# Which projection chains run beside the probability-times-V products, and when the first normalisation of a batch is put on VectorE

## The chip, the cores and the metric

The kernel runs on one core of one Trainium2 chip. The metric is device time in microseconds; the time before is the median of nine runs. One further run was recorded by the hardware profiler, and every view below comes from that run. The core has five engines with a queue of instructions each: TensorE (PE, with its weight loads shown apart as PEld), VectorE (DVE), ScalarE (ACT), GpSimd (POOL) and SyncE (SP, which here issues DMAs).

## The reference

Two independent problems, A and B, of the same shape, S = 2048 rows and D = 1024, 32 heads of 32, and a sliding window of 256 keys:

```python
qkv = (x @ wqkv).reshape(B, S, 3, H, Dh).transpose(2, 0, 3, 1, 4)
q, k, v = qkv[0], qkv[1], qkv[2]
scores = jnp.einsum("bhqd,bhkd->bhqk", q, k) * (Dh ** -0.5)
mask = (idx[:, None] - idx[None, :] >= 0) & (idx[:, None] - idx[None, :] < W)
p = softmax(jnp.where(mask, scores, -1e9))
o = jnp.einsum("bhqk,bhkd->bhqd", p, v)
return o.transpose(0, 2, 1, 3).reshape(B, S, D) @ wo
```

The two results are joined along the last axis. All inputs are bf16.

## The kernel before

**Work.** A group `g` is four heads (128 columns of Q or K), so there are 16 groups over both problems. Scores are made in units of 64 keys by 64 queries for the four heads at once, eight units to a *session*, which makes 152 sessions. A session (`session`) is a burst of score matmuls into one PSUM tile `st` of four banks (in array tiles of 32x64), then two exponentials on ScalarE, each over half of the banks (`exp(0)` and `exp(2)`, called "first half" and "second half" here), then masks on POOL (`diag`, and the far edge in place). There is one `st`, so the scores of the next session wait for both halves of this one.

Every second session (`PV_EVERY = 2`, the even ones from 4 on) is followed on TensorE by the products of probabilities with V for one to three blocks of 256 queries (`pv`), in array tiles of 128x32. A `pv` also multiplies by ones to get the row sums, and it reads a tile `both` that `edge` makes on VectorE by adding two masked pieces. The result sits in one of two PSUM buffers `acc` until it is normalised.

**A norm** is two pieces in a list `side`: a reciprocal of the sums (`rinv`), and then two shuffles, a multiplication into `oT` and for every second norm an OR into a running check word (`top`). `run_side` issues one piece. `finish_norm(keep)` issues pieces until no more than `keep` norms are open. It is called with 1 ahead of each `pv`, and with 0 in the session ahead of a session that has `pv` work. Otherwise `emit` issues a piece when its own rough clock of VectorE (`clock.dve`) is not ahead of TensorE's.

**Chains.** All dense products are *chains* that fill TensorE between sessions: `qk_steps` makes 512 columns of Q or K of a group (8 steps of N = 512), `v_steps` two blocks of V for two groups (16 steps of N = 256), `out_steps` a 128x512 piece of the output (8 steps of N = 512). A chain accumulates in one of two PSUM buffers `pp`, and its last step is followed by a copy out of PSUM on ScalarE or VectorE, whichever the rough clock has free first (`evacuate`). A chain has a first session in which it may start (`early`) and a session ahead of which it must be done (`late`); the list is sorted by `late`, `start_chain` takes the first that may start, `forced` finishes what is due, and `level` works out how much chain work each session gets so that the rest is spread evenly.

**Two forms of a step.** `by_columns` issues a step as one 128x128 matmul when `whole[0]` is true ("whole"), and otherwise as four matmuls of 32 columns each ("column-tiled"). `whole[0]` is false exactly in sessions with `pv` work, so that TensorE stays in the 128x32 tiling from `pv` through the chain work; it is true in the others. Line 197 is the whole form, line 201 the column-tiled one, line 511 the scores, 521 the exponentials, 559 the `edge` addition, 592 `pv`, 605 to 615 the norm, 220 and 222 the copies out of PSUM on ScalarE and VectorE.

**Order.** The order of instructions on each engine is that in which this program issues them; nothing reorders them afterwards.

Of the kernel before, what the change touches and what calls it, by code (L numbers as in the profile page):

```python
# [29 lines left out]
DG_BUFS = 5  # L30
X_AHEAD = 1
PV_EVERY = 2
VG = 2
NS_MM = 216.0
NS_ROW = 450.0
# [9 lines left out]
class _Cfg:  # L45
    def __init__(self, S, D):
        assert D % 512 == 0 and S % 512 == 0, (S, D)
        self.S, self.D = S, D
        self.CT = D // P
        self.T = D // P  # L50
        self.NB = S // P
        self.SC = S // 512
        self.NCH = D // 512
        self.NW = 512
        self.scale = float(DH) ** -0.5


class _Chain:
    def __init__(self, early, late, steps):
        self.early, self.late, self.steps = early, late, steps  # L60
        self.size = sum(ns for ns, _ in steps)


# [19 lines left out]
def _fast_path(ctx, tc, cfg, problems, outs, consts, certify):  # L83
# [5 lines left out]
    NP = NB // 2  # L89
    NM = NPROB * T // VG  # L90
    ones = consts["ones"]
# [81 lines left out]
    def new_wv(m):  # L173
        wv[m] = wvp.tile([P, CT, VG * P], BF16, name="wv")

    def load_wv(m, lo, hi, queue):
        pi, mm = divmod(m, T // VG)
        w_ = VG * P
        queue.dma_start(out=wv[m][:, lo:hi, :],
# [25 lines left out]
    whole = [True]  # L205
# [39 lines left out]
    def v_steps(m, b):  # L245
        pi = m // (T // VG)
        k, a = divmod(b, QB)
        st_ = {}
        steps = []
        w_ = VG * P  # L250
        for h in range(512 // w_):
            for ct in range(CT):
                def f(ct=ct, h=h):
                    if "pp" not in st_:
                        st_["pp"] = new_pp()
                        if (m, k) not in vts:
                            vts[(m, k)] = vp.tile([P, QB, w_], BF16, name="vt")
                    by_columns(st_["pp"], h * w_, (h + 1) * w_,
                               xT[(pi, k)][:, ct, (a + h) * P:(a + h + 1) * P],
                               wv[m][:, ct, :], ct == 0, ct == CT - 1)  # L260
                    clock.pe += NS_MM * w_ / 512.0
                    if ct == CT - 1 and h == 512 // w_ - 1:
                        evacuate(vts[(m, k)][:, a:a + h + 1, :],
                                 st_["pp"][:].rearrange("p (h w) -> p h w", w=w_))
                steps.append((NS_MM * w_ / 512.0, f))
        return steps
# [43 lines left out]
    def pv_time(g, p):  # L310
        return -(-(edge_time(g, p) + 1) // PV_EVERY) * PV_EVERY

# [83 lines left out]
    chains = []  # L396
    for g in range(G):
        for k in range(NQ):
            for which in (0, 1):
                if g == 0 and k == 0:  # L400
                    continue
                late = first_use(g, k, 1 - which) - (1 if g else 0)
                early = max(-(-(g - 1) * NE // SLOTS), landed("x", g // T, k), landed("wqk", g))
                chains.append(_Chain(early, late, qk_steps(g, which, k)))
    for m in range(NM):
        for b in range(0, NB, 512 // (VG * P)):
            k = b // QB
            early = max(0, landed("x", m * VG // T, k), landed("wv", m))
            if m > 1:
                early = max(early, pv_time(VG * (m - 1) - 1, min(2 * k + 2, NP - 1)) + 1)  # L410
            late = pv_time(VG * m, b // 2) if m or k else 1
            chains.append(_Chain(early, late, v_steps(m, b)))
    for pi in range(NPROB):
        final = pi == NPROB - 1
        for b in range(NB):
            k = b // QB
            for ch in range(cfg.NCH):
                early = max(pv_time(pi * T + T - 1, 2 * k + 1) + 1, landed("wo", pi, ch))
                late = FREE if final else wo_time[(pi + 1, ch)] - 1
                if not final and k < NPROB * NQ - (2 * NQ - 1):  # L420
                    late = pv_time((pi + 1) * T, 2 * (2 * NQ - 1 - NQ + k)) - 1
                steps = last_steps if (pi, b, ch) == (NPROB - 1, NB - 1, cfg.NCH - 1) else out_steps
# [10 lines left out]

    current = []

    def start_chain(now):
        for n, c in enumerate(chains):
            if c.early <= now:
                current.extend(chains.pop(n).steps)
                return True  # L440
        return False

    def run_side():
        cost, f, last = side.pop(0)
# [5 lines left out]
    def emit(now, budget):  # L450
        done = 0.0
        while (current or chains) and done < budget - 0.5 * (current[0][0] if current else NS_MM):
            if not current and not start_chain(now):
                break
            ns, f = current.pop(0)
            f()
            done += ns
            second_half(clock.pe > clock.act)
            if side and (clock.dve < clock.pe + 100.0 or len(side) > 8):
                run_side()  # L460
# [103 lines left out]
    def pv(g, p):  # L564
        pi, t = divmod(g, T)
        m, u = divmod(g, VG)
        k, h = divmod(p, QB // 2)
        dg = diags.pop((g, p))

        def old(us):  # L570
            return [(n * HALF, w_ * HALF, pts[s_][:, :, a * HALF:(a + w_) * HALF])
                    for s_, a, w_, n in runs(g, us)]

        mids = [old(parts(q - 1, q)) if q else [] for q in (2 * p, 2 * p + 1)]
        moves = []
        if p:
            moves += [(None, 2 * p - 2) + x for x in old(parts(2 * p - 2, 2 * p))]
            moves += [(None, 2 * p - 1) + x
                      for x in old(parts(2 * p - 1, 2 * p) + parts(2 * p - 1, 2 * p + 1))]
        moves += [(None, 2 * p, P + o, w_, src) for o, w_, src in mids[1]]  # L580
        moves += [(None, 2 * p + i, i * P, P, dg[:, :, i, :]) for i in range(2)]
        for i in range(2):
            moves += [(i, 0, 2 * P + o, w_, src) for o, w_, src in mids[i]]
        acc = ps_acc.tile([P, 512], F32, name="acc")
        clock.pe = max(clock.pe, clock.norms.pop(0))
        sums = edges.pop((g, p)) if p else dg
        moves += [(i, 0, 2 * P, P, sums[:, :, i, :]) for i in range(2)]
        for x, (h, j, o, w_, src) in enumerate(moves):
            for r in range(4):
                c = u * P + 32 * r  # L590
                lhsT = vts[(m, j // QB)][:, j % QB, c:c + 32] if h is None else ones[:, h, :]
                nc.tensor.matmul(acc[32 * r:32 * r + 32, o:o + w_], lhsT=lhsT,  # L592
                                 rhs=src[:, r, :], start=(x == 0), stop=(x == len(moves) - 1),
                                 tile_position=(0, 32 * r), skip_group_check=True)
            clock.pe += NS_PV * w_ / P
        if (pi, k) not in oTs:
            oTs[(pi, k)] = opool.tile([P, T, 512], BF16, name="oT")
        turn = g * NP + p
        wide = normp.tile([P, 256], F32, name="wide")
        pieces = []  # L600

        def f():
            if turn % 2 == 0:
                inverses[0] = normp.tile([P, 2, P], F32, name="rinv")
            nc.vector.reciprocal(out=inverses[0][:, turn % 2, :], in_=acc[:, 2 * P:3 * P])  # L605
        pieces.append((COST["rinv"], f, False))

        def f():
            for h in range(2):
                nc.vector.stream_shuffle(out=wide[:, h * P:(h + 1) * P], in_=inverses[0][:, turn % 2, :],  # L610
                                         mask=[16 * h] * 32)
            nc.vector.tensor_tensor(out=oTs[(pi, k)][:, t, (p % 2) * 256:(p % 2 + 1) * 256],  # L612
                                    in0=acc[:, 0:256], in1=wide[:], op=ALU.mult)
            if turn % 2:
                nc.vector.scalar_tensor_tensor(
                    out=top[:], in0=inverses[0][:].rearrange("p h q -> p (h q)").bitcast(I32),
                    scalar=IN_RANGE, in1=top[:], op0=ALU.bitwise_xor, op1=ALU.bitwise_or)
        pieces.append((COST["mult"] + (COST["or"] if turn % 2 else 0.0), f, True))
        n = max([i + 1 for i, x in enumerate(side) if x[2]], default=0)
        side[n:n] = pieces  # L620

    def finish_norm(keep=0):
        while sum(x[2] for x in side) > keep:
            run_side()
# [66 lines left out]
    for now in range(END):  # L691
        forced(now)
        whole[0] = not (due and due[0][0] <= now)
        session(now)
        while due and due[0][0] <= now:
            _, pg, pk = due.pop(0)
            finish_norm(1)
            pv(pg, pk)
        if due and due[0][0] == now + 1:
            finish_norm()  # L700
        while edges_due and edges_due[0][0] <= now:
            edge(*edges_due.pop(0)[1:])
        emit_all(now, level(now) - fixed[now])
# [230 lines left out]
```

## Time and profile before

| | |
|---|---|
| median of nine runs | 609.66 us (608.88 to 611.62) |
| the profiled execution, its own time | 610.67 us |
| its span in the profile | 608.9 us |
| TensorE matmul busy | 587.7 us, 97% |
| TensorE weight loads busy | 364.3 us, 60% |
| VectorE busy | 409.8 us, 67% |
| ScalarE busy | 412.1 us, 68% |
| GpSimd busy | 360.2 us, 59% |
| instruction fetches (queue q8) | 115 packets, 1.88 MB |

The profiled execution's time is 1.8 us above its span, which is what lies around the span. A matmul's duration in the profile is modelled and overlaps its neighbours, so a busy share of 97% does not mean that the array works at its peak for 97% of the time: the distance between the starts of two matmuls says what a step takes. Some matmul records are missing from the trace: 75 of the whole steps of N = 512 are in the program and not in the records, most of them the first one after a burst of scores.

### The profile page before, as it was taken

How to read it: one execution, taken by the hardware profiler on the slowest of the kernel's cores; microseconds unless marked ns; L12 is line 12 of the kernel's file. 1: busy time of each engine (PE TensorE's matmuls, PEld its weight loads, DVE VectorE, ACT ScalarE, POOL GpSimd, SP SyncE). 2: the span in 40 equal slices, each digit the busy share in tenths (PEclk: the TensorE clock that was granted, in tenths of full speed). 3: DMA queues.
4: the chain of work that ended last, by engine and by line, in shares of the span. 5: the costliest groups of instructions: out<-in, count | busy, mean ns of one | idle time of the engine just before them, and what ended most of it. 6: DMA issues, size and time to landing. Idle time of an engine off the chain costs nothing.

```text
span 608.9 us, 32535 instructions
## 1 busy us (share of the span) xinstructions
PE 587.7 (97%) x14364; PEld 364.3 (60%) x14439; DVE 409.8 (67%) x1144; ACT 412.1 (68%) x523; POOL 360.2 (59%) x918
## 2 busy tenths in 40 slices
PE   9999999999999999999999999999999999999996
PEld 6566566657655666665665766665555765555443
DVE  1288786887887867866577766766868776767200
ACT  3577867787778777786567766777767777765332
POOL 0477666766777676766466666665666666664000
PEclk9999999999999999999999999999999999999999
DMA  9915110111034102544211100112020030114222
GB/s 241 174 48 133 38 38 4 39 37 39 4 56 89 40 3 46 102 89 107 55 38 37 38 4 4 39 37 73 3 81 29 12 100 11 56 55 132 71 78 65
DMA packets 86820, 35.73 MB, mean 59 GB/s; under 512 B 65552, under 2 KB 86160, under 8 KB 86672
## 3 DMA queue, kind: packets, MB, share of 16 engines
q1 hardware_dynamic: 85632, 33.31, 22.4%
q8 instruction: 115, 1.88, 1.3%
q10 hardware_dynamic: 1040, 0.26, 0.2%
q14 instruction: 33, 0.27, 0.2%
HBM read 17.83 MB, written 8.39 MB: 43 GB/s over the span
## 4 chain that ended last, share of the span: by engine, by line
PE 65%; issue 1%; ACT 0%; DVE 0%; ACTq 0%
PE pp L197 31%; PE pp L201 19%; PE acc L592 8%; PE st L511 6%; ACT pt L521 0%; ACT osb L220 0%; DVE unsafe_i L888 0%; PE pp L887 0%; ACTq L220 0%; ACT kT L220 0%
## 5 line engine op out<-in xcount | busy, mean ns | idle before, releaser
L521 ACT ACTIVATE pt<-st 128x1024 bf16<-128x1024 f32 x304 | 302.2, 1026 | 107.0 <-PE st L511 56.4
L532 POOL TENSOR_SCALAR_AFFINE_SELECT diag<-pt 128x256 bf16<-128x256 bf16 x512 | 210.9, 436 | 196.4 <-ACT pt L521 179.9
L559 DVE TENSOR_TENSOR both<-diag,pt 128x512 bf16<-128x512 bf16 (+1 forms) x256 | 123.6, 525 | 55.1 <-PE acc L592 29.0
L545 POOL TENSOR_SCALAR_AFFINE_SELECT pt<-pt 128x512 bf16<-128x512 bf16 (+1 forms) x256 | 154.8, 623 | 0.0
L197 PE MATMUL pp<-xT,wqk 128*128 128x512 bf16 (+1 forms) x581 | 135.8, 373 | 6.5 <-issue 5.2
L605 DVE RECIPROCAL rinv<-acc 128x128 f32<-128x128 f32 x128 | 121.7, 951 | 26.8 <-PE acc L592 25.2
L201 PE MATMUL pp<-xT,wqk 128*32 128x512 bf16 x1608 | 97.1, 379 | 0.0
L197 PEld LDWEIGHTS <-wqk 128*128 128x128 bf16 x638 | 59.1, 98 | 62.3 <-issue 0.3
L197 PE MATMUL pp<-wo_sb,oT 128*128 128x512 bf16 (+1 forms) x349 | 77.7, 374 | 2.2 <-issue 1.6
L511 PEld LDWEIGHTS <-kT 32*64 32x64 bf16 x3904 | 41.8, 103 | 57.4 <-issue 55.8
L197 PE MATMUL pp<-wv,xT 128*128 128x256 bf16 x587 | 71.0, 273 | 0.4 <-issue 0.4
L511 PE MATMUL st<-qT,kT 32*64 32x64 bf16 (+4 forms) x3904 | 66.9, 236 | 1.6 <-issue 0.6
L610 DVE STREAM_SHUFFLE wide<-rinv 128x128 f32<-128x128 f32 x256 | 64.3, 296 | 0.0
L220 ACT CAST osb<-pp 128x512 bf16<-128x512 f32 (+1 forms) x61 | 35.4, 580 | 42.0 <-PE pp L197 28.7
L197 PEld LDWEIGHTS <-xT 128*128 128x128 bf16 x587 | 55.5, 98 | 11.9 <-issue 0.4
L201 PEld LDWEIGHTS <-wqk 128*32 128x32 bf16 x1608 | 42.0, 97 | 31.7 <-issue 0.4
L197 PEld LDWEIGHTS <-oT 128*128 128x128 bf16 x367 | 34.7, 98 | 39.6 <-issue 0.4
L201 PE MATMUL pp<-wv,xT 128*32 128x256 bf16 x1748 | 55.2, 273 | 2.3 <-issue 2.3
L612 DVE TENSOR_TENSOR oT<-acc,wide 128x256 bf16<-128x256 f32 x128 | 54.4, 425 | 4.4
L201 PEld LDWEIGHTS <-xT 128*32 128x32 bf16 x1748 | 46.2, 97 | 7.2 <-issue 3.3
L592 PE MATMUL acc<-pt,vt 128*32 128x128 bf16 (+2 forms) x1792 | 48.8, 223 | 0.0
L592 PEld LDWEIGHTS <-vt 128*32 128x32 bf16 x2816 | 43.5, 97 | 7.7 <-issue 0.4
(47 smaller groups left out, 387.4 us busy)
## 6 DMA issues: line engine op xcount, KB each, us to landing
out_dram<-osb SPq DMA_DIRECT2D x63, 128.0 KB, 1.9
wqk<-in_B_wqkv_dram SPq DMA_DIRECT2D x32, 128.0 KB, 3.3
wqk<-in_A_wqkv_dram SPq DMA_DIRECT2D x24, 128.0 KB, 3.0
wo_sb<-in_A_wo_dram SPq DMA_DIRECT2D x16, 128.0 KB, 2.8
wv<-in_B_wqkv_dram SPq DMA_DIRECT2D x16, 128.0 KB, 3.3
wo_sb<-in_B_wo_dram SPq DMA_DIRECT2D x16, 128.0 KB, 2.2
oT<-in_A_x_dram SPq DMA_DIRECT2D x4, 256.0 KB, 4.8
wv<-in_A_wqkv_dram SPq DMA_DIRECT2D x2, 512.0 KB, 5.6
```

Of the source, the lines that this page charges most:

```text
L197: nc.tensor.matmul(out[:, lo:hi], lhsT=lhsT, rhs=rhs, start=start, stop=stop, skip_group_check=True)
L201: nc.tensor.matmul(out[c:c + 32, lo:hi], lhsT=lhsT[:, c:c + 32], rhs=rhs, start=start, stop=stop, tile_position=(0, c), skip_group_check=True)
L220: nc.scalar.copy(out=out, in_=in_)
L511: nc.tensor.matmul(scores[c * HALF:(c + 1) * HALF, r, a * HALF:(a + w_) * HALF], lhsT=kT[rows, keys], rhs=qT[rows, q:q + w_ * HALF], start ...
L521: nc.scalar.activation(out=pt[:, lo:lo + 2, :n * HALF], in_=scores[:, lo:lo + 2, :n * HALF], func=ACT.Exp, bias=-SHIFT, scale=cfg.scale)
L532: nc.gpsimd.affine_select(out=diags[(g, p)][:, :, h, lo:lo + HALF], in_=pt[:, :, a * HALF:(a + 1) * HALF], pattern=[[0, 4], [1, HALF]], co ...
L545: nc.gpsimd.affine_select(out=blk, in_=blk, pattern=[[0, 4], [-1, w_ * HALF]], compare_op=ALU.is_gt, fill=0.0, base=-HALF * (us[a][2] - 3) ...
L559: nc.vector.tensor_tensor(out=both[:, :, h, o:o + w_], in0=dg[:, :, h, o:o + w_], in1=pts[t][:, :, a:a + w_], op=ALU.add)
L592: nc.tensor.matmul(acc[32 * r:32 * r + 32, o:o + w_], lhsT=lhsT, rhs=src[:, r, :], start=(x == 0), stop=(x == len(moves) - 1), tile_positi ...
L605: nc.vector.reciprocal(out=inverses[0][:, turn % 2, :], in_=acc[:, 2 * P:3 * P])
L610: nc.vector.stream_shuffle(out=wide[:, h * P:(h + 1) * P], in_=inverses[0][:, turn % 2, :], mask=[16 * h] * 32)
L612: nc.vector.tensor_tensor(out=oTs[(pi, k)][:, t, (p % 2) * 256:(p % 2 + 1) * 256], in0=acc[:, 0:256], in1=wide[:], op=ALU.mult)
```

## The change

A chain gets a mark, `dense`, which is set for V chains alone. When a chain is about to start, `start_chain` now looks at the session's form and at what is left of its budget. In a session with whole-array steps it wants a V chain as long as more than 900 ns of the budget are left, and otherwise one of the others; in a column-tiled session it is the other way round. If the first chain that may start is not of the wanted kind and is not due by the next session, the first one of the wanted kind that may start and is due within 14 sessions (`REACH`) is taken in its place. Apart from that, one call `finish_norm(1)` is put behind the `pv` batch of a session.

```diff
+REACH = 14
...
 class _Chain:
-    def __init__(self, early, late, steps):
-        self.early, self.late, self.steps = early, late, steps
+    def __init__(self, early, late, steps, dense=False):
+        self.early, self.late, self.steps, self.dense = early, late, steps, dense
...
-            chains.append(_Chain(early, late, v_steps(m, b)))
+            chains.append(_Chain(early, late, v_steps(m, b), dense=True))
...
-    def start_chain(now):
-        for n, c in enumerate(chains):
-            if c.early <= now:
-                current.extend(chains.pop(n).steps)
-                return True
-        return False
+    def start_chain(now, left):
+        able = [n for n, c in enumerate(chains) if c.early <= now]
+        if not able:
+            return False
+        pick = able[0]
+        want = whole[0] == (left > 900.0)
+        if chains[pick].late > now + 1 and chains[pick].dense != want:
+            pick = next((n for n in able if chains[n].dense == want
+                         and chains[n].late <= now + REACH), pick)
+        current.extend(chains.pop(pick).steps)
+        return True
...
-            if not current and not start_chain(now):
+            if not current and not start_chain(now, budget - done):
...
             _, pg, pk = due.pop(0)
             finish_norm(1)
             pv(pg, pk)
+        if not whole[0]:
+            finish_norm(1)
         if due and due[0][0] == now + 1:
             finish_norm()
```

## The prediction

> **What bounds the kernel now.** I read the chain of waits on the page first, then TensorE's groups by shape, then TensorE's timeline for the distance between starts, then the waits of the weight loads, and last VectorE's timeline wherever TensorE stood still.
>
> ```profile
> PE 65%; issue 1%; ACT 0%; DVE 0%; ACTq 0%
> ```
>
> The chain that ended last is TensorE's own work; no other engine holds 1% of it. So only two things count: what a TensorE step costs, and the places where TensorE stands still.
>
> The steps, in the order whole Q/K, whole V, column-tiled V, column-tiled Q/K:
>
> ```profile
> 200.64 1.89 PE L197 MATMUL pp<-xT,wqk 128*128 128x512 bf16 x8 [0.16 <-PE st L511]
> 202.37 0.93 PE L197 MATMUL pp<-wv,xT 128*128 128x256 bf16 x7
> ...
> 165.44 1.69 PE L201 MATMUL pp<-wv,xT 128*32 128x256 bf16 x53
> ...
> 293.69 2.00 PE L201 MATMUL pp<-xT,wqk 128*32 128x512 bf16 x32
> ```
>
> Columns: start, extent, what, how many. One V matmul lasts 273 ns in the profile, one of N = 512 379. Whole V: (930 - 273) / 6 = 109 ns a step. Column-tiled V: (1690 - 273) / 52 x 4 = 109 ns. Whole Q/K: (1890 - 379) / 7 = 216 ns. Column-tiled Q/K: (2000 - 379) / 31 x 4 = 209 ns (216 from start to start over all runs of such steps). The two forms cost the same. A change between score tiles and either form costs 92 to 94 ns, from starts, whatever chain follows.
>
> Now the places where TensorE stands still:
>
> ```profile
> PEld L201 <- issue: 4.1, 6, 1.3
> ...
> 204.76 0.93 PE L201 MATMUL pp<-wv,xT 128*32 128x256 bf16 x25
> 206.69 0.29 PE L201 MATMUL pp<-wv,xT 128*32 128x256 bf16 x3 [1.01 <-issue]
> ...
> 292.91 1.05 PE L201 MATMUL pp<-wv,xT 128*32 128x256 bf16 x31 [1.04 <-issue]
> ```
>
> "Issue" means that no semaphore held it. In TensorE's instruction order, the stop at 206.69 is 194 instructions past a multiple of 256. I measured the starts of all matmuls against the program's order: thirteen stops (101.8, 141.1, 154.4, 167.4, 206.7, 215.0, 234.6, 292.9, 303.1, 339.4, 405.9, 441.5, 522.8 us) lie at 194 or 195 past a multiple of 256, in V, scores and Q/K alike, and only the first has a semaphore too. Together they are 5.0 us. The DMA view between 203.32 and 206.69 us shows one packet on the instruction queue; all 115 packets are 16 KB or 256 instructions of 64 bytes. TensorE outran its instruction fetch.
>
> The other kind of stop is inside `pv`, eleven of them, together 2.8 us:
>
> ```profile
> 84.33 0.24 PE L592 MATMUL acc<-both,ones 128*32 128x128 bf16 x4 [0.18 <-DVE both L559]
> 84.87 0.24 PE L592 MATMUL acc<-both,ones 128*32 128x128 bf16 x4 [0.30 <-DVE both L559]
> ...
> 78.83 0.69 DVE L222 CAST vt<-pp 128x512 bf16<-128x512 f32 x1 [0.67 <-PE pp L201]
> 79.43 0.95 DVE L605 RECIPROCAL rinv<-acc 128x128 f32<-128x128 f32 x1
> ...
> 83.66 2.27 DVE L559 TENSOR_TENSOR both<-diag,pt 128x512 bf16<-128x512 bf16 x4
> ```
>
> `pv` waits for `both`, which VectorE makes late. One batch earlier VectorE sat 0.67 us on a copy whose chain was not done, with the first norm behind it; both norms then ran in the odd session ahead of the additions.
>
> **What the Trainium skill says.** "Runtime: NRT & Kernel Launch", section Instruction fetch mechanics: instructions stream in 16 KiB blocks of 256, the next fetched while the current one runs, the crossing "mostly hidden". The trace agrees on the block, but the crossing is not hidden where 256 instructions run in under about 3 us. "TensorE: Matmul & The Clock Gate", section Back-to-back issue gap: N / 2.4 + 2.5 ns, so 109 and 216; the trace agrees, in both forms. "TensorEngine Tiling (Array Packing)", Key Properties: a change of tiling drains the array (here 92 to 94 ns); its Restrictions: column tiling disables fast weight load. No rate here shows the latter, as the loads are hidden.
>
> **Part 1, the choice of chain.** The instruction orders of both kernels give the moves. V steps in whole form go from 587 to 772 of 1024, column-tiled from 437 to 252: 185 leave. Q/K column-tiled go from 402 to 500, output from 153 to 159: 104 enter. In plain step time this is worth nothing: 185 x (109 - 109) + 104 x (216 - 216). The changes of tiling stay as many.
>
> What it moves is instruction density. A column-tiled V step is 8 instructions in 109 ns, or 73 per us, a column-tiled Q/K step 37, a whole V step 18; `pv` is 146. TensorE loses 486 instructions. I added the durations of each block of 256 from boundary to boundary (109 and 216 per step, N / 2.4 + 2.5 by the number of tiles for scores and `pv`, 92 per change). Before, 16 blocks take under 3.0 us, and what all blocks lack of 3.25 us sums to 10.7 us; 5.0 us of that was really lost, since some fetches start early. After, 10 blocks are under 3.0, and the lack is 7.2. At the same share the loss is 7.2 x 5.0 / 10.7 = 3.4 us: **-1.7 us**. Bounds: -4 (the share falls, as fetches lie better) and +1.5 (as now at 292.9, where a block of 3.05 us lost 1.2 because its fetch began late).
>
> The choice also moves work in time. V chains come early, the sum of steps is up to 5.5 us ahead by session 20, and sessions 20 to 70 get less, about 0.11 us each and 0.22 from 57 to 69. The total is the same at session 70 and the order hardly differs from 140 on. A shorter session leaves ScalarE less room. Where a copy lies between the two halves, it needs 0.39 to the first half, 0.92 + 0.47 to the second, 1.03 for that and 0.05 back: 2.86 us, and more if the copy waits for its chain:
>
> ```profile
> 197.24 1.02 ACT L521 ACTIVATE pt<-st 128x1024 bf16<-128x1024 f32 x1 [0.61 <-ACT pt L521]
> 198.50 0.59 ACT L220 CAST vt<-pp 128x512 bf16<-128x512 f32 x1 [0.23 <-PE pp L201]
> 198.98 1.03 ACT L521 ACTIVATE pt<-st 128x1024 bf16<-128x1024 f32 x1
> ```
>
> Session 54 above is already bound: the next scores start at 200.06, 50 ns after the second half. Going through the sessions with these durations I get 0.47 us of such waits before (the trace has 0.45) and 0.85 after, in sessions 21, 23, 53, 54, 59, 63 and 69: **+0.4 us**, bounds 0.1 and 5.
>
> Third, chains other than V run closer to their use. Only one gets too close: K of group 0, block 3, is finished at the end of session 6 and read in the middle of the scores of session 7, 0.2 us after its last matmul. The like case today (Q block 1, session 1, 0.18 us) stops the scores for 0.65 us, so **+0.5 us**, bounds 0 and 0.8. All others keep 1.2 us or more. V of group pairs 2 to 4 starts 3 to 6 sessions sooner, in sessions 29, 47 and 66; the loads were issued at 63.7, 124 and 191 us, tens of us ahead, so SP's and POOL's queues hold nothing up.
>
> **Part 2, the norm behind the batch.** No work is added; the first of two norms moves ahead of the even session's addition and copies. It waits for the first `acc`, which is done half a batch (about 0.5 us) before; behind it wait an addition that is needed two sessions later, and copies, which go to ScalarE where the rough clock has VectorE behind. A norm is 1.86 us, 2.20 with its OR (200.82 to 203.02 in VectorE's timeline), an addition about 1.15. Between two batches VectorE then has 1.86 + 2.20 + 2 x 1.15 = 6.4 us against about 6.3 from the first `acc` to the use of `both`, with no copy to idle on. At each of the stops where two norms were open, the odd session's addition now has one norm in front instead of one and a half or two. I take 0.6 us of waits in place of 2.8: **-2.2 us**. Bounds: -2.8, and +1 if a late copy on VectorE keeps a `pp` buffer.
>
> **Sum.** -1.7 + 0.4 + 0.5 - 2.2 = -3.0. The profiled span goes from 608.9 to 605.9 and its own time from 610.67 to 607.7; the median shown is 1.0 below that run, so 606.7.
>
> **Rivals.** *ScalarE becomes the bound in sessions 20 to 70 (slower).* The shorter sessions fall under the chain first half, copy, second half. For it: today the margin there is often 50 to 300 ns and sessions lose 110 to 220. Against: only 20 sessions in the new order have a copy between the halves and are under 3.13 us. If all of them wait as copies do in session 54 (0.25 each), this costs 5.0 in place of 0.4, and the kernel ends 1.6 us slower, at 611.3. It decides from 3.4 us of such waits on, where the gain is gone.
>
> *Stops only change places (no change).* Which block is short depends on where boundaries fall, and a removed wait on `both` makes its block shorter: the blocks at 37, 75, 84 and 438 us were covered by such waits. Then fetch loses 5 again and some of the 2.2 comes back as fetch: 609.7. For it: the fetch at 292.9 was late for reasons outside TensorE. Against: the counted lack already has these blocks uncovered.
>
> *Nearly all stops go (much faster).* Fetch and `both` together are 7.8 us; with 7.0 of them gone and 0.9 paid, 603.6. Against: one block of 2.0 us remains in the new order.
>
> **Numbers.** My sum 0.52 (own range 604.5 to 608.4), much faster 0.12, no change 0.17, slower 0.19. About 0.2% (1.2 us) is what a measurement of this kernel can tell from no change. Faster takes 0.49 of the first and the 0.12: 0.61; same 0.03 + 0.14 = 0.17; slower 0.22, with the rest of the third. Range: 603.2, which takes in most of the much faster case, to 611.0, which leaves out the slower case's upper half.
>
> **What would show it.** Thirteen fetch stops fall to seven to ten, with 3 to 4 us; no stop of over 1 us in column-tiled V. Waits on `both` are under 1 us. VectorE's reciprocal follows `pv` with no copy ahead. A stop of about 0.5 us inside the scores near 44 us. Step distances stay at 109 and 216. I am wrong if whole V steps come out over 109 ns, if scores wait for ScalarE for over 2 us, or if the stops at block boundaries keep their 5 us.

## The result and the profile after

The changed kernel takes 607.31 us (median of ten runs, 606.39 to 608.15) against 610.31 us of the kernel before in the runs beside it: a ratio of 0.9951, 95% interval 0.9939 to 0.9964. The forecast was 3.0 us less, and 3.0 us less came. The profiled execution took 608.26 us with a span of 606.5 us. The same total hides a different split from the one forecast, so the match is in part luck (see below).

The page after, the chain that ended last and three groups (line numbers have moved by 1 to 8; columns as on the page before):

```profile
PE 58%; issue 2%; POOL 1%; DVE 1%; ACT 1%; ACTq 0%; POOLq 0%
...
L611 DVE RECIPROCAL rinv<-acc 128x128 f32<-128x128 f32 x128 | 121.8, 952 | 89.3 <-PE acc L598 89.3
...
L202 PE MATMUL pp<-xT,wqk 128*32 128x512 bf16 x2000 | 119.8, 379 | 0.1
L198 PE MATMUL pp<-wv,xT 128*128 128x256 bf16 x772 | 91.9, 273 | 1.4 <-issue 1.2
```

The chain that ended last is still TensorE's own work. The counts show that the change does what it says: 2000 column-tiled Q/K matmuls (500 steps) and 772 whole V steps. The reciprocal's line shows part 2. VectorE now sits in front of the reciprocal, waiting for the `acc` it reads, for 89.3 us in all (before: 25.2 of the 26.8 us that it idled there); the waiting that used to lie in front of the `both` additions (55.1 us, now 11.3) and of the copies (57.8, now 45.2) now lies in front of the norms. VectorE's timeline around a batch (start, duration, what, and in brackets the idle time before):

```profile
82.43 0.96 DVE L611 RECIPROCAL rinv<-acc 128x128 f32<-128x128 f32 x1 [1.76 <-PE acc L598]
...
84.31 0.95 DVE L611 RECIPROCAL rinv<-acc 128x128 f32<-128x128 f32 x1
...
86.62 1.42 DVE L565 TENSOR_TENSOR both<-diag,pt 128x512 bf16<-128x512 bf16 x4
```

Both norms start as soon as the first `acc` is there, with no copy ahead, and the additions follow. Inside `pv` only two waits on `both` are left, 0.49 us together, where there were eleven with 2.8.

The waits of the weight loads, though, show that one kind of stop has stayed:

```profile
PEld L202 <- issue: 5.2, 6, 1.8
PEld L198 <- issue: 1.5, 4, 0.6
```

TensorE's timeline holds the longest:

```profile
379.82 0.93 PE L202 MATMUL pp<-wv,xT 128*32 128x256 bf16 x27
382.23 0.61 PE L202 MATMUL pp<-wv,xT 128*32 128x256 bf16 x13 [1.48 <-issue]
```

No semaphore, column-tiled V, and 195 instructions past a multiple of 256. There are nine such stops in this execution with 4.9 us, where the forecast said 3.4. Two of them, here and at 291.13 us, are over 1 us and in column-tiled V, where the forecast had none.

The stop that was forecast for session 7 is there. All engines between 42.2 and 43.0 us:

```profile
42.20 0.32 PE L517 MATMUL st<-qT,kT 32*64 32x192 bf16 x12
...
42.32 0.58 ACT L221 CAST kT<-pp 128x512 bf16<-128x512 f32 x1 [0.90 <-PE pp L202]
...
42.96 0.32 PE L517 MATMUL st<-qT,kT 32*64 32x256 bf16 x8 [0.44 <-ACT kT L221]
```

The scores begin, meet a block of K whose copy has only just started, and lose 0.61 us, measured between the starts of matmuls.

All runs side by side. "Own time" is that of the profiled execution, to which the stops belong; "boundary stops" are those at 194 to 196 instructions past a multiple of 256 with nothing else to wait for, in us; those inside `pv` that also have a semaphore are counted under `both`. Only gaps of over 35 ns are counted. Each ratio is to the kernel before in runs of the same batch (medians 610.31 us beside the whole change; 609.69 beside norm_only, chains_only, norm_shift and after_shift; 609.55 beside the others), so medians of different batches are not to be subtracted to a tenth. A profiled execution need not be a typical one: those of norm_only, norm_shift, the whole change and after_shift42 were the slowest of their batch, those of after_shift and split the fastest.

| run | own time | median | ratio (95% interval) | boundary stops | waits on `both` | stop in session 7 |
|---|---|---|---|---|---|---|
| before | 610.67 | 609.66 | | 5.0 | 2.8 | |
| before_again | 609.40 | | | 4.6 | 2.8 | |
| whole change | 608.26 | 607.31 | 0.9951 (0.9939 to 0.9964) | 4.9 | 0.5 | 0.6 |
| after_again | 607.33 | | | 3.3 | 0.5 | 0.6 |
| norm_only | 611.10 | 608.15 | 0.9976 (0.9967 to 0.9985) | 8.5 | 0.5 | |
| norm_again | 609.10 | | | 6.5 | 0.2 | |
| chains_only | 608.23 | 608.97 | 0.9993 (0.9981 to 1.0005) | 2.1 | 3.7 | 0.6 |
| norm_shift | 611.21 | 608.43 | 0.9984 (0.9974 to 0.9993) | 8.5 | 0.7 | |
| after_shift | 604.18 | 605.28 | 0.9932 (0.9916 to 0.9948) | 1.4 | 0.6 | 0.6 |
| after_shift42 | 606.98 | 606.21 | 0.9941 (0.9928 to 0.9953) | 5.0 | 0.3 | 0.6 |
| split | 620.08 | 621.50 | 1.0207 (1.0189 to 1.0225) | 14.3 | 0.6 | 0.6 |
| inverted | 609.50 | 608.34 | 0.9977 (0.9968 to 0.9986) | 7.6 | 0.5 | |
| from7_shift | 604.36 | 604.07 | 0.9906 (0.9892 to 0.9920) | 1.9 | 0.4 | |

### The profile page after: what moved, and what is told of

Read it like the earlier page. It is cut to its first block, busy times and chain, and to the rows that moved or that the text cites. A ratio compares the mean times of both kernels' runs of the same rounds, so it can differ in the third digit from the quotient of the medians.

```text
span 606.5 us, 32035 instructions
## 1 busy us (share of the span) xinstructions
PE 585.3 (97%) x14123; PEld 362.2 (60%) x14196; DVE 401.6 (66%) x1134; ACT 416.5 (69%) x533; POOL 361.6 (60%) x918
## 4 chain that ended last, share of the span: by engine, by line
PE 58%; issue 2%; POOL 1%; DVE 1%; ACT 1%; ACTq 0%; POOLq 0%
PE pp L198 28%; PE pp L202 18%; PE acc L598 7%; PE st L517 5%; ACT pt L527 0%; POOL diag L538 0%; POOL pt L551 0%; DVE both L565 0%; DVE rinv L611 0%; DVE wide L616 0%; ACT kT L221 0%; DVE oT L618 0%; ACT osb L221 0%; DVE top L621 0%; POOL wqk L394 0%
## 5 line engine op out<-in xcount | busy, mean ns | idle before, releaser
L538 POOL TENSOR_SCALAR_AFFINE_SELECT diag<-pt 128x256 bf16<-128x256 bf16 x512 | 215.1, 445 | 192.5 <-ACT pt L527 175.8
L611 DVE RECIPROCAL rinv<-acc 128x128 f32<-128x128 f32 x128 | 121.8, 952 | 89.3 <-PE acc L598 89.3
L565 DVE TENSOR_TENSOR both<-diag,pt 128x512 bf16<-128x512 bf16 (+1 forms) x256 | 119.2, 509 | 11.3 <-POOL diag L538 5.8
L198 PE MATMUL pp<-xT,wqk 128*128 128x512 bf16 (+1 forms) x486 | 117.0, 372 | 5.7 <-issue 4.6
L202 PE MATMUL pp<-xT,wqk 128*32 128x512 bf16 x2000 | 119.8, 379 | 0.1
L198 PE MATMUL pp<-wv,xT 128*128 128x256 bf16 x772 | 91.9, 273 | 1.4 <-issue 1.2
L198 PEld LDWEIGHTS <-xT 128*128 128x128 bf16 x772 | 74.0, 98 | 15.7 <-issue 1.0
L198 PEld LDWEIGHTS <-wqk 128*128 128x128 bf16 x540 | 49.3, 98 | 49.0 <-issue 0.3
L202 PEld LDWEIGHTS <-wqk 128*32 128x32 bf16 x2000 | 51.7, 97 | 40.9 <-issue 1.2
L221 ACT CAST qT<-pp 128x512 bf16<-128x512 f32 x57 | 33.5, 587 | 18.4 <-PE pp L202 10.0
L221 ACT CAST vt<-pp 128x512 bf16<-128x512 f32 x48 | 28.3, 590 | 21.4 <-PE pp L202 12.8
```

The costliest lines, as they stand in the source:

```text
L198: nc.tensor.matmul(out[:, lo:hi], lhsT=lhsT, rhs=rhs, start=start, stop=stop, skip_group_check=True)
L202: nc.tensor.matmul(out[c:c + 32, lo:hi], lhsT=lhsT[:, c:c + 32], rhs=rhs, start=start, stop=stop, tile_position=(0, c), skip_group_check=True)
L221: nc.scalar.copy(out=out, in_=in_)
L538: nc.gpsimd.affine_select(out=diags[(g, p)][:, :, h, lo:lo + HALF], in_=pt[:, :, a * HALF:(a + 1) * HALF], pattern=[[0, 4], [1, HALF]], co ...
L565: nc.vector.tensor_tensor(out=both[:, :, h, o:o + w_], in0=dg[:, :, h, o:o + w_], in1=pts[t][:, :, a:a + w_], op=ALU.add)
```

## The experiments

**norm_only and chains_only: each part alone.** The first is the kernel before with only the new call, the second the change without it:

```diff
+        if not whole[0]:
+            finish_norm(1)
```

> Part 2 alone: the call behind the batch, with the chains chosen as before; TensorE's instructions are those of before, in the same order. Theory A (the gain is the norm's, the choice of chain brings nothing): the waits on both inside pv fall from 2.8 to about 0.5 us, the stops at block boundaries stay at about 5 us, the K of group 0 that was late in session 7 is not, and the time is 0.9950 to 0.9968 of before, not slower than the whole change. Rival B (both parts gain): 0.9970 to 0.9985, behind the whole change by 1 us or more.

> Part 1 alone: the new choice of chain, without the call behind the batch; TensorE's order is that of the whole change. Theory A: 0.999 to 1.004 of before: boundary stops of about 5 us as in the whole change, 0.6 us lost at session 7, 0.85 us of waits of scores for ScalarE, and some waits on both left. Rival B: 0.9965 to 0.9985.

Part 2 alone gives 0.9976, part 1 alone 0.9993, both together 0.9951. So neither theory holds in full. The waits on `both` went with part 2, as Theory A has it, but the time fell by less than they were worth (1.5 us by the ratio); in its profile the boundary stops are up at 8.5 us, although not one TensorE instruction had moved. One place shows how. TensorE's timeline of the kernel before:

```profile
84.87 0.24 PE L592 MATMUL acc<-both,ones 128*32 128x128 bf16 x4 [0.30 <-DVE both L559]
...
86.03 1.93 PE L201 MATMUL pp<-wv,xT 128*32 128x256 bf16 x64
87.89 0.42 PE L511 MATMUL st<-qT,kT 32*64 32x192 bf16 x20
```

and of norm_only:

```profile
84.73 1.92 PE L201 MATMUL pp<-wv,xT 128*32 128x256 bf16 x64
86.58 0.32 PE L511 MATMUL st<-qT,kT 32*64 32x192 bf16 x9
87.29 0.33 PE L511 MATMUL st<-qT,kT 32*64 32x64 bf16 x11 [0.40 <-issue]
```

Before, `pv` lost 1.3 us here to waits on `both`, and the 20 scores after the chain then ran through. Without these waits the same chain is done 1.3 us sooner, and the scores stop in the middle, at a block boundary, and lose 0.58 us. The wait had given the instruction fetch its time. Part 1 alone shows the reverse: its waits on `both` are 3.7 us, and its boundary stops only 2.1.

**before_again, norm_again and after_again: the same programs once more**, with no edit.

> The kernel before once more, for a second profile. The boundary stops were 5.0 us in an execution of 610.67 us. If their sum differs from one execution to the next, and is what makes the times of one program differ, the sum changes with this execution's own time, about 1 us for 1 us, and the waits inside pv stay at 2.5 to 3 us at the same places. If the stops are the same each time, 5.0 us within 0.5.

> Part 2 alone once more. Its profiled execution had 611.10 us, 3 us above its median, with 9 us of boundary stops. If the stops vary between executions, one near the median of 608.15 has about 6 us: still more than the kernel before at its median (about 4), since the waits inside pv no longer cover the fetch. If the uncovering is only chance, 4 us or less near 606.5.

> The whole change once more. Its profiled execution had 608.26 us, 1 us above its median, with 4.9 us of boundary stops, so about 4 us at 607.3 and 1 us of stops more or less for each us of its own time. Waits inside pv 0.5, the stop at session 7 0.6, scores for ScalarE 0.8, all as before, since TensorE's, VectorE's and ScalarE's orders alone set them.

The waits on `both`, the stop in session 7 and the scores' waits for ScalarE came back within 0.05 us for the kernel before and the whole change. The boundary stops did not: norm_only went from 8.5 to 6.5 us when the own time went from 611.10 to 609.10, the whole change from 4.9 to 3.3 when it went from 608.26 to 607.33, the kernel before only from 5.0 to 4.6 for 1.3 us, less than expected. So the stops of one program differ from one execution to the next, and go with a good part of the spread of its times. (norm_only was profiled on another chip than norm_again, so the chip may have a share in their difference.) In both pairs of profiles the order is the same: part 2 alone has about 3.4 us more of them (8.5 against 4.9, 6.5 against 3.3) than the whole change. That is what part 1 is for. By the times the fetch gain is less, about 2.6 us: the whole change is 1.5 us below part 2 alone, and part 1 pays 0.6 us in session 7 and 0.5 in waits for ScalarE.

**split: twice the instructions for the same streaming.**

```diff
-                    by_columns(st_["pp"], h * w_, (h + 1) * w_,
-                               xT[(pi, k)][:, ct, (a + h) * P:(a + h + 1) * P],
-                               wv[m][:, ct, :], ct == 0, ct == CT - 1)
+                    for lo in ((0,) if whole[0] else (0, P)):
+                        hi = w_ if whole[0] else lo + P
+                        by_columns(st_["pp"], h * w_ + lo, h * w_ + hi,
+                                   xT[(pi, k)][:, ct, (a + h) * P:(a + h + 1) * P],
+                                   wv[m][:, ct, lo:hi], ct == 0 and lo == 0, ct == CT - 1)
```

> The whole change, but each column-tiled V step of N = 256 is issued as two of N = 128 side by side: the same streaming (111.7 against 109.2 ns a step by N / 2.4 + 2.5, 0.6 us over 252 steps), twice the instructions (16 a step), 2016 more in all. Theory C (a dense stretch outruns the instruction fetch): blocks of 256 under 3.0 us go from 8 to 16 and what blocks lack of 3.25 us from 6.8 to 18 us, so the boundary stops rise from 4.9 us to between 9 and 16, most of them in column-tiled V, and the time is 612 to 620 us. Rival D (fetch that starts late for reasons outside TensorE decides, density does not): 607.5 to 609 us, stops of 4 to 6 us.

The median is 621.5 us, 14 us above the whole change; the boundary stops are 14.3 us, 12.5 of them in column-tiled V. The expectation's upper end for the time was 620. The waits of the weight loads and TensorE's timeline:

```profile
PEld L202 <- issue: 13.8, 14, 1.9
```

```profile
388.60 0.51 PE L202 MATMUL pp<-wv,xT 128*32 128x128 bf16 x23
389.96 1.97 PE L202 MATMUL pp<-wv,xT 128*32 128x128 bf16 x128 [0.86 <-issue]
393.44 0.23 PE L202 MATMUL pp<-wv,xT 128*32 128x128 bf16 x1 [1.50 <-issue]
```

Between the last two stops stand 128 matmuls, with their weight loads exactly one block of 256 instructions: 1.8 us of work from first start to last, in 3.48 us of time. With the distance of an unhindered V step at 2 x 56 ns, density makes this loss without a late fetch (the like stop at 296.34 us is 1.7 us, and its fetch began 0.7 us after the boundary), and Rival D falls for dense stretches.

**inverted: the choice turned round.**

```diff
-        want = whole[0] == (left > 900.0)
+        want = whole[0] != (left > 900.0)
```

> The whole change with the choice of chain turned round: V is wanted in column-tiled sessions (735 of 1024 V steps column-tiled, where the change has 252 and the kernel before 437), Q, K and output in whole ones. The norm's call stays. Theory C: lack of the blocks 11 us against 6.8, boundary stops of 6 to 10 us, step distances unchanged at 109 and 216 ns, no late K in session 7, 608.5 to 612 us. Rival E (a V step in column-tiled form costs more by itself): 483 more such steps show a distance over 112 ns, and the time grows with their number. Rival F (the choice of chain is worth nothing): as part 2 alone, 0.9976 of before.

With 735 column-tiled V steps the distance of a step is still 109 ns in both forms, so Rival E falls: the form costs nothing by itself. The time, 608.34 us and 0.9977 of before, is below Theory C's window and equals part 2 alone, as Rival F had it. (That the choice as made is worth nothing doesn't follow: the whole change's interval lies below that of part 2 alone.) The boundary stops, 7.6 us, lie in its window and between the two profiles of part 2 alone. The count of lack had said 11 against 10.6 us, so the two are not told apart here.

**norm_shift, after_shift and after_shift42: only the boundaries move.** In norm_shift and after_shift, nine of the warming matmuls at the start become 72 narrow ones; in after_shift42 only the three before `first(0, 0)` become 24.

```diff
-            nc.tensor.matmul(warm[:], lhsT=blank[:, 0:P], rhs=blank[:, 0:512], start=True, stop=True)
+            nc.tensor.matmul(warm[:, 0:w_], lhsT=blank[:, 0:P], rhs=blank[:, 0:w_], start=True,
+                             stop=True)
...
-    keep_warm(6)
+    keep_warm(6, 64)
...
-    keep_warm(3)
+    keep_warm(3, 64)
```

> Part 2 alone, and nine of the warming matmuls at the start become 72 of an eighth of the columns, so 126 more instructions stand ahead of everything and every boundary of 256 falls 126 instructions earlier in the work; nothing else moves. Summed over blocks, what they lack of 3.25 us falls from 10.6 to 6.3 us. Theory C (the stops are instruction fetch, set by where dense stretches lie against the boundaries): the stops move to the new boundaries, none stays at its old place, and their sum falls from 5 to about 3 us, so about 2 us less than part 2 alone, 0.991 to 0.9945 of before. Rival D (the stops belong to a place in the work, or the start of a fetch decides and not the density): sum stays within 1 us of 5, time within 1 us of part 2 alone.

> The whole change with the same 126 instructions more at the start; lack of the blocks falls from 6.8 to 3.3 us. Theory C: boundary stops fall from 4.9 to 2.4 us, time 0.989 to 0.993 of before. Rival D: 0.9935 to 0.997, as the whole change, with stops at new places that sum to 4 to 6 us.

> A control for after_shift: the whole change with 42 more instructions at the start (three warming matmuls made 24 small ones), which moves the boundaries by 42 and leaves the summed lack at 6.5 us against 6.8. If the sum of lacks sets the loss: as the whole change, 0.994 to 0.9965 of before. If small matmuls at the start gain by themselves, or any move of the boundaries does: as after_shift, 0.9932 or less.

In all three the stops moved with the boundaries: they are again 194 or 195 past a multiple of 256, now in other places of the work. That the stops belong to boundaries and not to places in the work is therefore shown. Their sum is another matter. For the whole change it went the way that was counted, 1.4 us and a median of 605.28, and in the control 5.0 us and 606.21; but the ratio, 0.9932, lies between the windows of Theory C and Rival D, the intervals of the whole change, the control and after_shift overlap, and the stops are those of after_shift's fastest execution and the control's slowest. So it is not shown that one shift is better than the other. For part 2 alone Theory C missed: the count fell from 10.6 to 6.3 us, the stops stayed at 8.5 (again in the slowest execution) and the time at that of norm_only. Adding up what blocks lack of 3.25 us foretells large differences, as in split, and not ones of this size.

One thing these runs do show: part 1's gain is no lucky place of the boundaries. With the boundaries where they were, the whole change is 1.5 us below part 2 alone (0.9951 against 0.9976), and with both moved by 126 instructions 3.2 us (0.9932 against 0.9984), with intervals apart both times.

**from7_shift: the choice from session 7 on, and the boundaries moved.** The shift is that of after_shift; beside it:

```diff
-        if chains[pick].late > now + 1 and chains[pick].dense != want:
+        if now > 6 and chains[pick].late > now + 1 and chains[pick].dense != want:
```

> The whole change with the choice of chain only from session 7 on, so that the K chain that was late keeps its old place, and with the 126 instructions more at the start. The 0.6 us stop at session 7 goes; waits of scores for ScalarE 1.2 us by my count against 0.85; lack of the blocks 4.3 against 3.3 us in after_shift. Theory C with these sums: 605 to 606 us, the same as after_shift (605.3) within 1 us. If the late K is worth its 0.6 us alone: 604.7.

604.07 us, 0.9906 of before: the best of all and clear of the whole change by its interval. Its median is 1.2 us below after_shift, in another batch, and their intervals overlap (0.9892 to 0.9920, 0.9916 to 0.9948). The stop of session 7 is gone; boundary stops are 1.9 us. This is nearer to the second of the two expectations (604.7) and beyond it; what the late K is worth alone can't be read from this time.

**The fetched packets: why a block stops.** The traces hold the time of every packet on the instruction queue (q8). Packet n belongs to the stop 194 or 195 instructions past n x 256. The first view below is a block of the kernel before, 203.32 to 206.69 us, that ended in a stop. The second and third are stretches of the whole change, one behind the other: 199.57 to 201.57 us, the end of one block, and 201.57 to 203.53 us, the whole of the next (40 slices to a stretch):

```profile
DMA  0000000090000000000000000000000000000000
q8 instruction: 1, 0.02, 2.5%
...
DMA  0000090000000000000000000000000000000000
q8 instruction: 1, 0.02, 4.3%
...
DMA packets 0, 0.00 MB, mean 0 GB/s; under 512 B 0, under 2 KB 0, under 8 KB 0
```

In the first, the packet starts 0.7 us after the boundary and takes 1.3 us (2.5% of 16 x 3.37), and TensorE goes on 1.3 us after the packet's end. The block of the third view takes 1.96 us in all and doesn't stop: its packet had started in the block ahead, 1.7 us before the boundary. So it is in all thirteen traces. No boundary was crossed sooner than 1.1 us after the end of its packet, and the 104 stops of 0.3 us or more with no semaphore ended 1.1 to 1.6 us after it. A stop is therefore the time by which packet and delay outlast the block's work. The prediction's "under about 3 us" is a rule for fetches that start soon after the boundary: blocks of 2 us ran through where the fetch was early, and blocks with 3.1 to 3.9 us of work stopped where it began 2.0 us after the boundary (at 242.56, 258.45 and 291.13 us in the whole change). Density and the start of the fetch both count; the second is the true part of Rival D.

## Why the prediction was right, and which of its terms was not

- **What bounds the kernel: right.** Step distances are 109 and 216 ns in both forms in every run here (split's halves apart), and the differences between kernels are in the main differences of stops.
- **Part 2, -2.2 us: the mechanism and the size right.** Waits on `both` went from 2.8 to 0.49 us, which is -2.3. The reason given, the copy in front of the first norm, is what VectorE's timeline shows gone. What the step left out is that these waits covered the fetch: alone, part 2 brought 1.5 us. In this the rival "Stops only change places" was right.
- **The fetch term, -1.7 us: this is the step that failed in its size.** The first pair of profiles gives -0.1 (5.0 to 4.9), the second -1.3 (4.6 to 3.3). The prediction's own sign of being wrong, that the stops "keep their 5 us", came true in the first. The failing step is "At the same share the loss is 7.2 x 5.0 / 10.7". The share was taken from a kernel in which waits on `both` covered short blocks. The rival "Stops only change places" had named those blocks, and the answer given there, "the counted lack already has these blocks uncovered", is true of the 10.7 but not of the 5.0: with the waits gone, the same order lost 6.5 to 8.5 us. So part 1's gain in fetch is larger than put, 2.6 us by the times and about 3.4 by the profiles against part 2 alone, and most of it pays for what part 2 uncovers.
- **Scores waiting for ScalarE, +0.4 us: right.** Six waits of over 50 ns with 0.83 us (my sum: seven with 0.85), where the kernel before had two with 0.33. The rival that ends slower did not come.
- **The late K, +0.5 us: right,** 0.61 us in both profiles, and gone in from7_shift.
- **The sum: in part luck.** With -0.1, +0.5, +0.6 and -2.3 the stops of the first pair account for 1.3 us, and those of the second pair for 2.5, where the forecast had 3.0; the measured gain is 3.0 with an interval of 2.2 to 3.7. Of the 2.4 us by which the first profiled span fell, 1.1 are not in these stops. The first session's scores started 0.5 us sooner in that execution; after_again started as late as the kernel before, so this belongs to the execution. About 0.6 us stays unassigned.
- **The price of a step: right, but not as cited.** The Trainium skill's page "TensorE: Matmul & The Clock Gate", section Back-to-back issue gap, gives N / 2.4 + 2.5 ns for one matmul by itself, and about 131 ns per matmul of N = 512 for a sustained stream. Here such steps follow one another every 216 ns in every run, so in this case the formula holds for the stream and the 131 ns do not.

Why the fetch starts early for one block and late for another, and differently from one execution to the next, was not settled. In the stretch from 233 to 291 us, while x of problem B is loaded, several fetches began about 2 us after the boundary; no run took that load away.

## What to carry to other kernels

When a profile shows TensorE idle with no semaphore to blame, count instructions and look at the instruction queue's packets: stops at the same remainder of a block that end a fixed time after a packet are instruction fetch. What helped here was fewer instructions per microsecond; twice as many in column-tiled V cost 14 us. A wait that is removed may have been giving time to a second limit, so a change that lowers that limit (here the choice of chains) can look worthless alone and still be worth having beside the other. VectorE's in-order queue gained here by putting first what is ready first: the norm moved ahead of copies whose chains were not done.

## What the runs showed of the hardware

- TensorE's instructions come in blocks of 256, one 16 KB packet each. In all thirteen traces no boundary was crossed sooner than 1.1 us after the end of its packet, and the stops of 0.3 us or more with no semaphore ended 1.1 to 1.6 us after it. Their packets took 0.9 to 1.9 us.
- How long a block must last without a stop depends on when its fetch starts. Most of these stops (79 of 104) had a fetch that began up to 1.2 us after the boundary, and took 2.4 to 4.2 us from boundary to boundary; the block from 286.8 us in the whole change, whose fetch began after 2.0 us, took 4.4 us. Blocks of 1.96 and 1.97 us (to 203.5 and 482.1 us in the whole change) ran through, with fetches that had begun 1.7 and 2.2 us before them.
- The size of a stop at one and the same boundary differs between executions: in column-tiled V near 292 us the kernel before lost 1.21 us in one execution and 0.32 in the other.
- Weight loads in column-tiled form (four of 97 ns for one step of 109 ns) slowed no step in any run, from 252 to 735 such steps.
